# An early exponential for ScalarE's table, logits on two queues, halved matmuls in one half batch, and the last relus on VectorE, in a block-sorted attention with a top-1 expert layer

## The chip, the cores and the metric

The kernel runs on one core of one Trainium2 chip. The metric is the device time of one execution in microseconds (us). The kernel before took 153.61 us, the median of 3 runs (153.49 to 153.71). The profile shows one further execution, whose span from the first to the last instruction is 152.0 us.

## What is computed

The reference has two stages. The first is an attention in which the keys and values of each head are mixed over 8 blocks of 96 positions by a matrix P; P comes from five rounds of exponential, row normalisation and column normalisation of small logits (`sort_net`). The second sends each of the 3072 rows of the result to the one expert with the largest logit.

```python
B, H, S, D = 4, 8, 768, 64          # batch, heads, positions, head size
P = sort_net                        # (4, 8, 8, 8)
for _ in range(5):
    P = np.exp(P - np.max(P, axis=-1, keepdims=True))
    P = P / (np.sum(P, axis=-1, keepdims=True) + 1e-09)
    P = P / (np.sum(P, axis=-2, keepdims=True) + 1e-09)
k_sorted = einsum('bhij,bhjcd->bhicd', P, k_blocks)      # the same for v
attn = softmax(q_block @ k_sorted_block.T / sqrt(D))
x = (attn @ v_sorted_block)         # to (3072, 512)
logits = x @ w_gate                 # 8 experts
for e in range(8):                  # rows whose largest logit is e
    h = np.maximum(x[rows] @ w1[e], 0)                   # 512 -> 1024
    out[rows] = gate[rows] * (h @ w2[e])                 # 1024 -> 512
```

## The kernel before

The kernel does not write its instructions in a fixed order. It describes them as tasks, each with an assumed cost, the engines that could do it, its predecessors and a priority. A small planner inside the program places the tasks when the program is built: it assigns each to an engine and a time, tries 1500 random changes of the priorities from a fixed seed, keeps the changes that do not make the planned end later, and then emits the instructions in the order that it found. The program that reaches the chip is static. A changed cost or a changed choice of engine therefore changes the input of this search, and with it perhaps the order of every engine's instructions.

The planner guesses one expert for each batch ahead of time (a "vote" of summed values times the gate weights), so that this expert's weights can be loaded early; a branch after the last instruction repairs rows that went elsewhere, if there are any.

Where the plan leaves TensorE idle in the first 32 us, it puts in matmuls on a tile of zeros, whose results nobody reads:

```python
    def fill(self, t):
        at = self.free.get("pe", self.begin)
        while t.start < self.until and t.start - at > 0.5:
            n = self.grain if at < self.warm else 512
            free = [i for i in range(8) if self.bank[i] is not None and self.bank[i] <= at - 0.3]
            if not free:
                break
            t.spares.append((free[-1], n))
            ...
    # when the task is emitted
    for i, n in t.spares:
        nc.tensor.matmul(out=psum[:, i, :n], lhsT=idle[:, :128], rhs=idle[:, :n], start=True, stop=True)
```

The planner also counts TensorE's instructions, a matmul and its weight load as two, because it expects them to be fetched in blocks of 256 (`BLOCK_AT, BLOCK = 191, 256`), and it avoids runs of short instructions that would outpace the fetch.

The sort logits are loaded twice, into two groups of 32 partitions, both times from the sync queue; the gate weights come on ScalarE's queue. The five rounds then alternate between ScalarE (exponential) and VectorE (sum, reciprocal, product, once by rows and once by columns):

```python
    def load_sn(e, g):
        nc.sync.dma_start(out=sn[g * BH:(g + 1) * BH], in_=sort_net.rearrange("b h i j -> (b h) i j"))

    sn_at = [add(f"load sn{g}", {"sp": 0.4}, lambda e, g=g: load_sn(e, g), prio=-999, lands=0) for g in range(G)]
    wg_at = add("load wg", {"act": 1.75}, lambda e: nc.scalar.dma_start(
        out=wg32, in_=moe_w_gate.rearrange("(c p) e -> p c e", p=P)), prio=-998, lands=0)
    ...
    mk_idle = add("idle", {"dve": 0.27}, lambda e: nc.vector.memset(idle, 0.0), prio=-995)
    ...
    last = sn_at[0]
    for it in range(5):
        last = add(f"exp {it}", {"act": 0.26}, lambda e: nc.scalar.activation(sn, sn, ACT.Exp), [last, *sn_at], prio=-990)
        ...
        norm(sn, sn, it, "r")
        norm(sn.transpose([0, 2, 1]), sn.transpose([0, 2, 1]) if it < 4 else None, it, "c")
```

The end of the rounds (`sng`) gives the small matrices `pv0` and `pk0` with which TensorE sorts the values (16 groups of 32 matmuls in all, `v{b}.{g}`) and the keys (`k{b}.{g}`) of a batch. For the first batch the values are first rewritten in another order ("relay") by ScalarE, GpSimd or VectorE. The scores of a batch (`s`) need all of its query and key evictions, the products with the values (`a`) also those of the values.

```python
    t = add(f"k{b}.{g}", {"pe": 0.465}, run_k, [k_at[b][g], pk_at[b, 0], pk_at[b, 1], pads["ksT", i2], *scores_of.get(b - 2, [])], at,
            opens=kb, mode="col", n=16)
    ...
    ts = add(f"s{b}.{i}", {"pe": 0.178}, run_s, [*q_ev, *k_ev, ex_user[xi], pads["ex", xi]], ...)
    te = add(f"exp{b}.{i}", {"act": 0.82}, ...)
    ...
    later["vote pick0"].behind = later["k0.0"]      # the first batch's vote stands behind its first key sort
```

The expert layer of a half batch (384 rows) is 8 groups of 4 matmuls with 384 columns, each followed by a relu on ScalarE or VectorE, and then 3 tiles of 8 matmuls with 512 columns, each weighed by ScalarE or VectorE and stored. The first half of the first batch is cut into parts of 192 rows, and the very last tile of all into two halves of 256 columns.

```python
    def mm_outputs(ps, w2t, hT, s, lo, hi, d0=0, d1=MD):
        for fc in range(lo, hi):
            nc.tensor.matmul(out=ps, lhsT=hT[:, fc, s * P:(s + 1) * P], rhs=w2t[:, fc, d0:d1],
                             start=(fc == 0), stop=(fc == FC - 1))

    def relu(e, dst, src):
        if e == "act":
            nc.scalar.activation(dst, src, ACT.Relu)
        else:
            nc.vector.tensor_scalar_max(dst, src, 0.0)
    ...
    relus[r].append(add(f"relu{b}.{half}.{fc}.{r}", {"act": 0.5, "dve": 0.56}, ...))
```

Of the kernel before, what the change touches and what calls it, by code (L numbers as in the profile page):

```python
# [9 lines left out]
F32 = mybir.dt.float32  # L10
# [5 lines left out]
ACT = mybir.ActivationFunctionType  # L16
# [22 lines left out]
class Plan:  # L39
# [7 lines left out]


    FETCH = (3.9, 6.0)
    RING = 8  # L50
    BLOCK_AT, BLOCK, PACE, WAIT = 191, 256, 12.5, 300

# [12 lines left out]
    def add(self, name, cost, run, after=(), prio=0, opens=None, closes=None, lands=None,  # L65
            mode="full", n=0):
        t = Task(name, cost, run, after, prio, opens, closes, lands, mode, n)
        self.tasks.append(t)
        return t
# [43 lines left out]
    def fill(self, t):  # L113

        at = self.free.get("pe", self.begin)
        while t.start < self.until and t.start - at > 0.5:
            n = self.grain if at < self.warm else 512
            free = [i for i in range(8) if self.bank[i] is not None and self.bank[i] <= at - 0.3]
            if not free:
                break  # L120
            t.spares.append((free[-1], n))
            at += n * (0.00085 if at < self.warm else 0.00042)
            self.bank[free[-1]] = at - 0.3
# [191 lines left out]
def kernel(  # L315
# [11 lines left out]
    nc = tc.nc  # L327
    B, H, S, D = q.shape
    NB = sort_net.shape[-1]
    BLK = S // NB  # L330
    BH = B * H
    N, MD = out.shape
    E = moe_w_gate.shape[-1]
    F = moe_w1.shape[-1]
    P = 128
    DC = MD // P
    FC = F // P
# [9 lines left out]
    SUB = NH // P  # L347
# [9 lines left out]
    def bank(banks):  # L357
        return psum[:, banks.at, :]
# [5 lines left out]
    add = plan.add  # L364

    def sb(shape, dt, name):
        return consts.tile(shape, dt, name=name)
# [17 lines left out]
    w2s = [sb([P, FC, MD], BF16, f"w2_{i}") for i in range(2)]  # L385
    hTs = [sb([P, FC, NH], BF16, f"hT{i}") for i in range(3)]
    outs = sb([P, 4, MD], F32, "o")
    idle = sb([P, 512], BF16, "idle")

    G = 2  # L390
    sn = sb([G * BH, NB, NB], F32, "sn")
# [4 lines left out]
    wg = sb([P, DC, E], BF16, "wg")  # L396
# [37 lines left out]
    q_at, k_at, v_at, w1_at, w2_at = {}, {}, {}, {}, {}  # L434
# [30 lines left out]
    PIECES = 4  # L465
# [12 lines left out]


    def load_sn(e, g):  # L480
        nc.sync.dma_start(out=sn[g * BH:(g + 1) * BH], in_=sort_net.rearrange("b h i j -> (b h) i j"))

    plan.free["sp"], plan.free["act"] = 0.45, 0.9
    sn_at = [add(f"load sn{g}", {"sp": 0.4}, lambda e, g=g: load_sn(e, g), prio=-999, lands=0) for g in range(G)]
    wg_at = add("load wg", {"act": 1.75}, lambda e: nc.scalar.dma_start(
        out=wg32, in_=moe_w_gate.rearrange("(c p) e -> p c e", p=P)), prio=-998, lands=0)

    plan.free["pool"] = 1.4
# [4 lines left out]
    for t in FIRST_LOADS:  # L493
# [3 lines left out]
                  prio=FIRST + 4)  # L497
# [83 lines left out]
    ek1 = add("expand k", {"pool": 0.82}, lambda e: run_expand(expand_k, NB * CQ), [mk_ident], prio=FIRST + 10)  # L581
    ev1 = add("expand v", {"pool": 0.5}, lambda e: run_expand(expand_v, NB * 2), [mk_ident], prio=FIRST + 10)

    last = sn_at[0]
    for it in range(5):
        last = add(f"exp {it}", {"act": 0.26}, lambda e: nc.scalar.activation(sn, sn, ACT.Exp), [last, *sn_at], prio=-990)

# [408 lines left out]
            nc.tensor.matmul(out=ps, lhsT=w1t[:, dc, fc * P:(fc + 1) * P],  # L996
                             rhs=x[:, dc], start=(dc == 0), stop=(dc == DC - 1))

    def mm_outputs(ps, w2t, hT, s, lo, hi, d0=0, d1=MD):
        for fc in range(lo, hi):  # L1000
            nc.tensor.matmul(out=ps, lhsT=hT[:, fc, s * P:(s + 1) * P], rhs=w2t[:, fc, d0:d1],  # L1001
                             start=(fc == 0), stop=(fc == FC - 1))

    def relu(e, dst, src):
        if e == "act":
# [12 lines left out]


    TWICE = 20  # L1020
    FFN_BANKS, PARTS = None, 2

    def add_expert(b):
        A = SPAN * (b + 1)
        i2 = b % 2
        relu_of[b], outs_of[b] = [], []
        hs = []
        for half in range(2):
            hi = counts["hT"] % 3
            counts["hT"] += 1  # L1030
            hs.append(hi)
            parts = PARTS if b == half == 0 else 1
            n = NH // parts
            group = min(512 // n, 4)
            relus = [[] for _ in range(parts)]
            for r, fc in ((r, fc) for r in range(parts) for fc in range(0, FC, group)):
                pb = Banks(1, FFN_BANKS)
                lo = half * NH + r * n
                steps = NB // 2 // parts
                s0 = half * NB // 2 + r * steps  # L1040
                at = A + half * 50 + 25 * (r * FC + fc) / FC / parts

                def hidden(pb, n=n, group=group):
                    return bank(pb)[:, :group * n].rearrange("p (g n) -> p g n", g=group)

                def run_h(e, pb=pb, lo=lo, n=n, fc=fc, group=group, hidden=hidden):
                    for g in range(group):
                        mm_hidden(hidden(pb)[:, g], w1s[i2], columns(b, lo, n), fc + g)

                t = add(f"h{b}.{half}.{fc}.{r}", {"pe": group * (0.65 / parts + 0.015 * (parts > 1))}, run_h,  # L1050
                        [*w1_at[b][:2 if b == 0 and fc + group <= FC // 2 else PIECES], *turn_of[b][s0:s0 + steps], *(hT_user[hi] or [])],
                        at, opens=pb, n=group * DC)
                relus[r].append(add(f"relu{b}.{half}.{fc}.{r}", {"act": 0.5, "dve": 0.56},
                                 lambda e, fc=fc, hi=hi, pb=pb, r=r, n=n, group=group, hidden=hidden: relu(
                                     e, hTs[hi][:, fc:fc + group, r * n:(r + 1) * n], hidden(pb)),
                                 [t], at - 12, closes=pb))
            cut = len(relus[0]) // 2
            relu_of[b] += [t for got in relus for t in got]
            users = []
            for s in range(SUB):  # L1060
                t = half * SUB + s
                need = relus[s * P // n:((s + 1) * P - 1) // n + 1]
                oi = counts["o"] % 4
                counts["o"] += 1
                final = b == B - 1 and t == NTB - 1
                cuts = ((0, MD // 2, "act", "act"), (MD // 2, MD, "dve", "sp")) if final else ((0, MD, None, "sp"),)
                used = []
                for j, (lo, hi_, way, queue) in enumerate(cuts):
                    pb = Banks(1, FFN_BANKS)
                    us = 0.866 * (hi_ - lo) / MD  # L1070
                    t1 = add(f"o{b}.{half}.{s}a{j}", {"pe": us}, lambda e, s=s, hi=hi, pb=pb, lo=lo, hi_=hi_: mm_outputs(
                        bank(pb)[:, :hi_ - lo], w2s[i2], hTs[hi], s, 0, FC // 2, lo, hi_),
                        [*w2_at[b][:PIECES // 2], *[t for got in need for t in got[:cut]]], A + half * 50 + 25 + 25 * s / SUB, opens=pb, n=FC // 2)
                    t2 = add(f"o{b}.{half}.{s}b{j}", {"pe": us}, lambda e, s=s, hi=hi, pb=pb, lo=lo, hi_=hi_: mm_outputs(
                        bank(pb)[:, :hi_ - lo], w2s[i2], hTs[hi], s, FC // 2, FC, lo, hi_),
                        [t1, *w2_at[b][PIECES // 2:], *[t for got in need for t in got[cut:]]], A + half * 50 + 25 + 25 * s / SUB, n=FC // 2)
                    users.append(t2)
                    outs_of[b].append(t2)
                    cost = {e: c for e, c in evac(hi_ - lo, act=0.25 + (hi_ - lo) * 0.00086,
                                                  dve=0.2 + (hi_ - lo) * 0.00107).items() if way in (None, e)}  # L1080
                    tv = add(f"w{b}.{t}.{j}", cost, lambda e, lo=lo, hi_=hi_, oi=oi, t=t, pb=pb: weigh(
                        e, outs[:, oi, lo:hi_], bank(pb)[:, :hi_ - lo], gws[:, b, t:t + 1]),
                        [t2, route_at[b], *(out_user[oi] or [])], A + half * 50 + 25 * s / SUB, closes=pb)
                    dma = nc.scalar if queue == "act" else nc.sync
                    pieces = 2 if b * NTB + t < TWICE else 1

                    def run_st(e, lo=lo, hi_=hi_, oi=oi, t=t, dma=dma, pieces=pieces):
                        rows = P // pieces
                        for r in range(pieces):
                            dma.dma_start(out=out[out_rows(b, t), lo:hi_][r * rows:(r + 1) * rows],  # L1090
                                          in_=outs[r * rows:(r + 1) * rows, oi, lo:hi_])

                    used.append(add(f"st{b}.{t}.{j}", {queue: 0.36 * pieces}, run_st, [tv], A, lands=-(hi_ - lo) / MD / 4))
                out_user[oi] = used
            hT_user[hi] = users
# [50 lines left out]
        rest_i, bank(tot)[:, :1], -1.0, float(N), op0=ALU.mult, op1=ALU.add), [t2], 30, closes=tot)  # L1146


    spot = sb([1, 1], F32, "spot")
    for i in range(6):  # L1150
        add(f"spare dve{i}", {"dve": 0.5}, lambda e: [nc.vector.memset(spot, 0.0) for _ in range(8)],
            [route_at[B - 1]], SPAN * B + 55 + 5 * i)

    plan.search(rounds=1500, seed=7)
# [8 lines left out]
    with tc.If(rv > 0):  # L1163
        w1t, w2t, hT = w1s[0], w2s[0], hTs[0]
# [59 lines left out]
```

## Time and profile before

| Engine | busy, us | share of the span | instructions |
|---|---|---|---|
| TensorE matmuls | 140.8 | 93% | 2236 |
| TensorE weight loads | 96.7 | 64% | 2254 |
| VectorE | 88.0 | 58% | 270 |
| ScalarE | 99.7 | 66% | 160 |
| GpSimd | 67.2 | 44% | 127 |

In the profile PE is TensorE's matmuls, PEld its weight loads, DVE is VectorE, ACT ScalarE, POOL GpSimd and SP the sync engine; a letter q after a name is the engine's sequencer or queue. "L586" is line 586 of the kernel. A row of the timeline gives the start, the duration (of the whole merged row), the engine, the line, the operation, the tiles written and read, the number of instructions, and in square brackets how long the engine had been idle and what ended that wait. A row of the table by stretches gives the bounds and length of the stretch, the busy time and the instructions of the five engines, then the mean granted clock of TensorE as a share of the full one, the busy share of the DMA engines (its scale can pass 1), and GB/s.

Two things about the reading. The ends of matmuls are modelled, so a busy TensorE need not be a TensorE at its peak, and starts are the safer quantity. And a share of the whole span says little here, for the first 26 us and the remaining 126 us have different limits.

### The profile page before, as it was taken

To read this page: it belongs to the slowest core of one execution; us is meant where nothing else is said; L and a number is where in the kernel's file an instruction comes from. 1 tells how busy PE (TensorE), PEld (TensorE's weight loads), DVE (VectorE), ACT (ScalarE), POOL (GpSimd) and SP (SyncE) were. 2 spreads that over 40 slices of the span, in tenths; PEclk is the share of its full clock that TensorE was granted. 3 is DMA by queue.
4 is the path that set the end of the run, shared out by engine and by line. 5 is a ranking of instruction groups with operands and counts; after the bars stand their busy time and mean duration, and the time that the engine had idled before them with its cause. 6 is when DMAs were issued, how large, how long until landed. Compare 5 with 4: busy or idle time off the path is not lost. (4 is left out here: it accounts for less than half of the span.)

```text
span 152.0 us, 5435 instructions
## 1 busy us (share of the span) xinstructions
PE 140.8 (93%) x2236; PEld 96.7 (64%) x2254; DVE 88.0 (58%) x270; ACT 99.7 (66%) x160; POOL 67.2 (44%) x127
## 2 busy tenths in 40 slices
PE   6875998999999999999999999999999999999980
PEld 6653976995676567777557656967466566654550
DVE  1688848794674778768808657856053853552010
ACT  1838799863678979767488753868677465773440
POOL 6886099828892486992821990580000000000000
PEclk9999689999999999999999999999999999999999
DMA  2999079999999999999999999599953003331632
GB/s 25 184 214 201 14 95 164 205 220 206 217 239 236 249 213 240 233 228 223 213 208 246 257 206 229 103 162 196 195 121 71 4 0 73 69 73 69 137 134 80
DMA packets 15035, 24.52 MB, mean 161 GB/s; under 512 B 2080, under 2 KB 8224, under 8 KB 15008
## 3 DMA queue, kind: packets, MB, share of 16 engines
q0 software_dynamic: 10464, 17.83, 65.5%
q1 hardware_dynamic: 3872, 6.18, 14.9%
q8 instruction: 18, 0.29, 0.7%
q10 hardware_dynamic: 672, 0.15, 0.4%
q14 instruction: 9, 0.07, 0.1%
HBM read 35.68 MB, written 6.29 MB: 276 GB/s over the span
## 5 line engine op out<-in xcount | busy, mean ns | idle before, releaser
L996 PE MATMUL psum<-xT,w 128*128 128x384 bf16 (+1 forms) x288 | 48.4, 308 | 0.0
L1001 PE MATMUL psum<-w,hT 128*128 128x512 bf16 (+1 forms) x185 | 43.6, 370 | 1.2 <-issue 0.5
L1006 ACT ACTIVATE hT<-psum 128x384 bf16<-128x384 f32 x54 | 26.5, 491 | 12.9 <-PE psum L996 12.2
L996 PEld LDWEIGHTS <-w 128*128 128x128 bf16 x288 | 24.8, 97 | 12.1
L1001 PEld LDWEIGHTS <-hT 128*128 128x128 bf16 x200 | 18.2, 98 | 17.5
L1012 ACT ACTIVATE o<-psum,gws 128x512 f32<-128x512 f32 (+1 forms) x23 | 15.6, 678 | 20.4 <-PE psum L1001 18.4
L913 ACT ACTIVATE ex<-psum 128x768 bf16<-128x768 f32 x32 | 24.4, 810 | 0.8 <-PE psum L904 0.5
L931 DVE TENSOR_TENSOR xo<-psum,rec 96x512 bf16<-96x512 f32 x32 | 22.0, 686 | 1.1
L476 POOL DMA_DIRECT2D w<-in_moe_w_dram x16 | 11.7, 741 | 8.3 <-DVE xo L931 3.7
L425 ACT CAST vs<-psum 128x1024 bf16<-128x1024 f32 x12 | 12.2, 1019 | 2.9 <-PE psum L871 2.6
L930 DVE RECIPROCAL rec<-psum 96x8 f32<-96x8 f32 x32 | 6.4, 200 | 12.6 <-PE psum L920 12.3
L920 PEld LDWEIGHTS <-ex 128*128 128x128 bf16 x256 | 10.8, 97 | 3.3 <-ACT ex L913 0.6
L920 PE MATMUL psum<-vs,ex 128*128 128x65 bf16 x256 | 12.5, 193 | 0.4 <-ACT ex L913 0.2
L471 POOL DMA_DIRECT2D w<-in_moe_w_dram x16 | 9.5, 599 | 7.4 <-issue 4.8
L759 POOL TENSOR_TENSOR v_tmp<-vr 128x384 bf16<-128x384 bf16 x12 | 11.1, 959 | 1.4 <-DVE vr L737 1.4
L427 DVE COPY xT<-psum 128x384 bf16<-128x384 bf16 x22 | 7.8, 353 | 6.3 <-PE psum L939 5.7
L871 PE MATMUL psum<-pv,vr 128*64 128x64 bf16 x512 | 11.2, 203 | 0.0
L871 PEld LDWEIGHTS <-vr 128*64 128x64 bf16 x512 | 10.1, 118 | 1.5 <-issue 1.3
L427 DVE CAST ksT<-psum 128x1024 bf16<-128x1024 f32 (+1 forms) x7 | 8.0, 1146 | 4.7 <-PE psum L837 2.8
L939 PE MATMUL psum<-ident,xo 96*128 96x96 bf16 x128 | 10.6, 206 | 0.0
L939 PEld LDWEIGHTS <-xo 96*128 96x128 bf16 x128 | 8.1, 97 | 3.5
L129 PE MATMUL psum<-idle 128*128 128x80 bf16 (+1 forms) x76 | 8.5, 291 | 1.9 <-DVE idle L504 1.4
(110 smaller groups left out, 168.3 us busy)
## 6 DMA issues: line engine op xcount, KB each, us to landing
w<-in_moe_w_dram POOLq DMA_DIRECT2D x32, 256.0 KB, 9.0
out_dram<-o SPq DMA_DIRECT2D x41, 128.0 KB, 4.0
q_in<-in_q_dram POOLq DMA_DIRECT2D x4, 768.0 KB, 13.2
v_in<-in_v_dram POOLq DMA_DIRECT2D x4, 768.0 KB, 11.1
k_in<-in_k_dram POOLq DMA_DIRECT2D x3, 768.0 KB, 17.3
k_in<-in_k_dram POOLq DMA_DIRECT2D x3, 256.0 KB, 11.3
out_dram<-o SPq DMA_DIRECT2D x3, 256.0 KB, 2.6
out_dram<-o ACTq DMA_DIRECT2D x1, 128.0 KB, 3.4
```

The costliest lines, as they stand in the source:

```text
L425: nc.scalar.copy(dst, src)
L427: engines[e].tensor_copy(dst, src)
L476: nc.gpsimd.dma_start(out=w2s[i][:, at], in_=w2_r[bass.ds(ev, 1), :, at].rearrange("e p c d -> p (e c) d"))
L871: nc.tensor.matmul(out=t[f * HP:(f + 1) * HP, u, :], lhsT=vr[i2][:, d // 2, :, d % 2], rhs=pv[b][:, f * H:(f + 1) * H, :].rearrange("p h i ...
L913: te = add(f"exp{b}.{i}", {"act": 0.82}, lambda e, ex=ex, sbk=sbk: nc.scalar.activation(ex[:, :H * BLK].rearrange("p (t c) -> p t c", t=2) ...
L920: nc.tensor.matmul(out=av[:, h // 4, h % 4, :], lhsT=ex[:, h * BLK:h * BLK + P], rhs=vs[i2][:, h * NB + i, :D + 1], start=(h % 4 == 0), st ...
L931: nc.vector.tensor_mul(xo, av[:, :, :, :D], rec.to_broadcast([BLK, 2, 4, D]))
L939: nc.tensor.transpose(out=tp[:, dc, :], in_=xf[:, dc * P:(dc + 1) * P], identity=ident[:BLK, :BLK])
L996: nc.tensor.matmul(out=ps, lhsT=w1t[:, dc, fc * P:(fc + 1) * P], rhs=x[:, dc], start=(dc == 0), stop=(dc == DC - 1))
L1001: nc.tensor.matmul(out=ps, lhsT=hT[:, fc, s * P:(s + 1) * P], rhs=w2t[:, fc, d0:d1], start=(fc == 0), stop=(fc == FC - 1))
L1006: nc.scalar.activation(dst, src, ACT.Relu)
L1012: nc.scalar.activation(dst, src, ACT.Copy, scale=gw)
```

## The change

It has five parts.

1. A one-element exponential, which needs only the zeroed tile, is put ahead of the five rounds, so that ScalarE loads its table for the exponential while the logits are still on their way.
2. The second copy of the logits is started from ScalarE's queue instead of the sync queue, and the gate weights move to the sync queue.
3. The planner fills gaps of TensorE from 0.35 us on, instead of 0.5 us.
4. In the second half of the third batch (`SHORT = (2, 1)`), each matmul of 512 columns of the second expert product becomes two of 256.
5. The relus of the last batch may only go to VectorE. (The small tile `spot`, which fillers of VectorE at the end wrote, now belongs to part 1; those fillers write into the zero tile.)

```diff
+    GAP = 0.35
...
-        while t.start < self.until and t.start - at > 0.5:
+        while t.start < self.until and t.start - at > self.GAP:
...
-        nc.sync.dma_start(out=sn[g * BH:(g + 1) * BH], in_=sort_net.rearrange("b h i j -> (b h) i j"))
+        (nc.scalar if g else nc.sync).dma_start(out=sn[g * BH:(g + 1) * BH], in_=sort_net.rearrange("b h i j -> (b h) i j"))
...
-    sn_at = [add(f"load sn{g}", {"sp": 0.4}, lambda e, g=g: load_sn(e, g), prio=-999, lands=0) for g in range(G)]
-    wg_at = add("load wg", {"act": 1.75}, lambda e: nc.scalar.dma_start(
+    sn_at = [add(f"load sn{g}", {"act" if g else "sp": 0.4}, lambda e, g=g: load_sn(e, g), prio=-999, lands=0) for g in range(G)]
+    wg_at = add("load wg", {"sp": 0.4}, lambda e: nc.sync.dma_start(
...
-    last = sn_at[0]
+    spot = sb([1, 1], F32, "spot")
+    last = add("exp table", {"act": 1.5}, lambda e: nc.scalar.activation(spot, idle[:1, :1], ACT.Exp), [mk_idle], prio=-997)
...
-    def mm_outputs(ps, w2t, hT, s, lo, hi, d0=0, d1=MD):
+    def mm_outputs(ps, w2t, hT, s, lo, hi, d0=0, d1=MD, pieces=1):
+        n = (d1 - d0) // pieces
         for fc in range(lo, hi):
-            nc.tensor.matmul(out=ps, lhsT=hT[:, fc, s * P:(s + 1) * P], rhs=w2t[:, fc, d0:d1],
-                             start=(fc == 0), stop=(fc == FC - 1))
+            for i in range(pieces):
+                nc.tensor.matmul(out=ps[:, i * n:(i + 1) * n], lhsT=hT[:, fc, s * P:(s + 1) * P],
+                                 rhs=w2t[:, fc, d0 + i * n:d0 + (i + 1) * n],
+                                 start=(fc == i == 0), stop=(fc == FC - 1 and i == pieces - 1), skip_group_check=pieces > 1)
...
+    SHORT = (2, 1)
...
-                relus[r].append(add(f"relu{b}.{half}.{fc}.{r}", {"act": 0.5, "dve": 0.56},
+                relus[r].append(add(f"relu{b}.{half}.{fc}.{r}", {"dve": 0.56} if b == B - 1 else {"act": 0.5, "dve": 0.56},
...
+                short = 2 if b == SHORT[0] and half == SHORT[1] else 1
...                 # in t1 and t2: mm_outputs(..., short) and n=FC // 2 * short
...
-        add(f"spare dve{i}", {"dve": 0.5}, lambda e: [nc.vector.memset(spot, 0.0) for _ in range(8)],
+        add(f"spare dve{i}", {"dve": 0.5}, lambda e: [nc.vector.memset(idle[:1, :1], 0.0) for _ in range(8)],
```

More of the change, by code (lines that the diff above doesn't have):

```diff
@@ L1071, in add_expert @@
                     t1 = add(f"o{b}.{half}.{s}a{j}", {"pe": us}, lambda e, s=s, hi=hi, pb=pb, lo=lo, hi_=hi_: mm_outputs(
-                        bank(pb)[:, :hi_ - lo], w2s[i2], hTs[hi], s, 0, FC // 2, lo, hi_),
-                        [*w2_at[b][:PIECES // 2], *[t for got in need for t in got[:cut]]], A + half * 50 + 25 + 25 * s / SUB, opens=pb, n=FC // 2)
+                        bank(pb)[:, :hi_ - lo], w2s[i2], hTs[hi], s, 0, FC // 2, lo, hi_, short),
+                        [*w2_at[b][:PIECES // 2], *[t for got in need for t in got[:cut]]], A + half * 50 + 25 + 25 * s / SUB, opens=pb, n=FC // 2 * short)
                     t2 = add(f"o{b}.{half}.{s}b{j}", {"pe": us}, lambda e, s=s, hi=hi, pb=pb, lo=lo, hi_=hi_: mm_outputs(
-                        bank(pb)[:, :hi_ - lo], w2s[i2], hTs[hi], s, FC // 2, FC, lo, hi_),
-                        [t1, *w2_at[b][PIECES // 2:], *[t for got in need for t in got[cut:]]], A + half * 50 + 25 + 25 * s / SUB, n=FC // 2)
+                        bank(pb)[:, :hi_ - lo], w2s[i2], hTs[hi], s, FC // 2, FC, lo, hi_, short),
+                        [t1, *w2_at[b][PIECES // 2:], *[t for got in need for t in got[cut:]]], A + half * 50 + 25 + 25 * s / SUB, n=FC // 2 * short)
                     users.append(t2)
@@ L1146 @@
         rest_i, bank(tot)[:, :1], -1.0, float(N), op0=ALU.mult, op1=ALU.add), [t2], 30, closes=tot)
-    spot = sb([1, 1], F32, "spot")
     for i in range(6):
-        add(f"spare dve{i}", {"dve": 0.5}, lambda e: [nc.vector.memset(spot, 0.0) for _ in range(8)],
+        add(f"spare dve{i}", {"dve": 0.5}, lambda e: [nc.vector.memset(idle[:1, :1], 0.0) for _ in range(8)],
             [route_at[B - 1]], SPAN * B + 55 + 5 * i)
```

## The prediction, made before the changed kernel ran

> **What bounds the kernel now.** I read the table by stretches first, cut where the work changes, because the shares of the page mix a start that waits with a long stretch that does not.
>
> ```profile
> 6.10:16.40 10.30, 7.44 (x148) 5.00 (x150) 8.78 (x37) 6.54 (x13) 6.92 (x23) 1.00 1.01 187
> 16.40:19.80 3.40, 3.23 (x95) 3.27 (x96) 1.90 (x6) 2.40 (x3) 1.13 (x2) 0.50 0.02 5
> 19.80:26.10 6.30, 5.33 (x141) 4.07 (x139) 4.67 (x9) 6.17 (x9) 6.17 (x11) 1.00 1.01 140
> 26.10:147.70 121.60, 120.45 (x1801) 80.11 (x1814) 70.33 (x211) 81.83 (x134) 48.32 (x80) 1.00 0.84 170
> 147.70:152.00 4.30, 0.01 (x1) 0.00 (x0) 0.48 (x1) 0.00 (x0) 0.00 (x0) 1.00 0.35 118
> ```
>
> From 26.1 us, where the first expert matmul starts, to 147.7 TensorE is busy 120.45 of 121.60 us, and a few tenths of the rest are records that the trace lacks. Nothing else comes near: ScalarE has 81.83, VectorE 70.33. After that stand 4.30 us of last eviction and store. So the time is: when TensorE gets enough work to stay full, plus the work that is then left, plus a tail of 4.3 us. The change acts on the first term. In the start TensorE is busy for 7.44 of 10.30 us, dummies included; then come 3.40 us at half the clock (the column 0.50).
>
> What delays the start is seen in the timeline of the first 21 us and the waits before its rows:
>
> ```profile
> 1.00 0.86 SPq L481 DMA_DIRECT2D sn<-in_sort_net_dram  x2
> ...
> 3.31 1.28 ACT L586 ACT_TABLE_LOAD   x1 [3.31 <-DMA sn<-in_sort_net_dram]
> ...
> 4.60 0.26 ACT L586 ACTIVATE sn<-sn 64x64 f32<-64x64 f32 x1
> ...
> 12.23 0.76 PE L748 MATMUL psum<-vmask,v_in 128*128 128x8 bf16 x24
> ...
> 13.92 0.45 DVE L604 TENSOR_TENSOR sng<-sn,red 32x32 bf16<-32x32 f32 x2
> ...
> 14.43 0.24 PE L691 MATMUL psum<-sng,ev_first 64*128 64x8 bf16 x4 [1.44 <-DVE sng L604]
> ...
> 15.62 0.49 PEld L837 LDWEIGHTS <-k_in 128*64 128x64 bf16 x16
> ...
> 19.11 0.95 PE L837 MATMUL psum<-pk,k_in 128*64 128x128 bf16 x16
> ```
>
> The table load stands between the logits' landing (3.31) and the first exponential (4.60): 1.28 us on a serial chain. The chain ends with `sng` at 13.92 + 0.45 = 14.37, 9.77 us after its first exponential. TensorE waits 1.44 us for it and then does the value and key sorts at once. The third key sort stands at 19.11, the first scores at 21.01, the first expert matmul at 26.16.
>
> **What the Trainium skill says.** "ScalarE: Activation LUTs", section "What ACT_TABLE_LOAD costs", gives about 1283 ns for a load, and a drain of about 1380 ns more. This trace agrees on the first (1.28 us) and shows no drain: the exponential starts 0.01 us after the load. The exponential of the change needs the same set, so the load is moved, not added. "DMA: Bandwidth & Descriptors", section "Issuing engines are not separate DMA queues", says that starting transfers from several engines saves only the time of issuing them. Here that is half of 0.86 us. "TensorE: Matmul & The Clock Gate", section "What's actually happening", has a clock that is halved after a poorly used window of about 3.4 us. The trace fits: the clock falls at 16.37 us for 3.41 us, and in the 3.41 us before it the table by stretches has TensorE busy for only 1.97; the window before that, with 3.13, was followed by the full clock. "Runtime: NRT & Kernel Launch", section "Instruction fetch mechanics", has instructions fetched in blocks of 256. The page agrees in size: 18 packets on the instruction queue are 0.29 MB, so 16 KB each.
>
> **Part 1 and 2, the table and the queues.** The zero tile is ready at 1.12 + 0.27 = 1.39. ScalarE issues its copy of the logits from 1.00 to about 1.45, then loads the table until 1.45 + 1.28 = 2.73, and the tiny exponential may take 0.2 (the one of 64 elements takes 0.26): free at about 2.95. The logits: one transfer lands 1.7 us after its issue, so both are there at about 2.75 instead of 1.46 + 1.75 = 3.2. The first exponential moves from 4.60 to about 3.0, **1.6 us earlier**. If the rounds keep their 9.77 us, `sng` is done at 12.8. Then 14.37 no longer bounds; two transfers do. The values land at 12.2 (matmul at 12.23, released by the DMA). The three key copies are issued from 3.47 to 5.63 and land 10.9 to 11.6 us after their issue, so at about 14.4, 15.5 and 16.5. The first key sort can move from 15.65 to some 14.4, the third from 19.11 to some 16.6.
>
> The vote stands behind the first key sort, so it gains about 1.2 us, and the first expert's weights with it (issued at 18.67, the first pieces landed 4.3 to 4.8 us later, so by 24.2; then by 23.0). They were not the last to come: the transposed rows were evicted at 25.16 + 0.48 = 25.64. Those follow the first scores, and these follow the third key sort and its eviction (0.59 to 0.69): 16.6 + 0.35 + 0.65 = 17.6 at the earliest. But ScalarE and VectorE also have the other evictions and the relays then. From 12.2 on I count for ScalarE two relays (1.7), two value and two key evictions (2.0 + 1.6), and for VectorE from 12.8 on the small products (0.8), the vote (0.6), one query (1.2), two key (1.9) and one or two value evictions (1.2 to 2.4): they are done at about 17.5 and 18.5 to 19.7. So I put the first scores at 18.5 to 19, **2 to 2.5 us** ahead of 21.01.
>
> **Part 3, the dummies.** With the wait of 1.44 us gone or filled, the window before 16.37 should be used well enough, and the half clock should vanish. At half clock 3.41 us lost at most 1.7 us of TensorE's work, but this is no second gain: it lies inside the interval just counted, where evictions and landings set the pace (ScalarE waited 1.0 us there for TensorE, VectorE 1.8). It is what lets the 2 to 2.5 be had. A dummy of 512 columns costs 0.22 us if it meets ready work.
>
> **Part 4, halved matmuls.** 3 tiles x 8 = 24 matmuls become 48. In the last stretch of the trace, starts of 512-column matmuls lie 216 ns apart and those of 256 columns 109.5, so a pair costs 219: 24 x 3 ns = **0.07 us lost**. What it buys is position: 48 instructions more (a weight load with each) move the later fetch boundaries. In the kernel before I find no stall at a boundary worth more than 0.1 us after 26 us, so I credit nothing.
>
> **Part 5, the last relus.** A relu of 384 columns takes 0.49 us on ScalarE and 0.55 on VectorE. 16 of them leave ScalarE, at most 7.9 us, and make 8.9 us on VectorE, which is nearly idle at the end (9.23 us of wait before its last instruction). TensorE waited for neither there. Each relu is 0.06 us later, hidden behind other matmuls: zero, and the tail of 4.3 us stays.
>
> **Sum.** The long stretch begins 2 to 2.5 us earlier, with about the same work left; minus 0.07; minus what the plan gives back, since its search starts from other numbers. In the long stretch the old plan lost hardly anything that is visible, so a new one is likelier a little worse: 0.2 us or so. I choose a gain of 2.0: 153.6 - 2.0 = **151.6 us**.
>
> **Rivals.** (a) *The landings take the place of the table.* Keys land at 16.5 whatever ScalarE does, so if the evictions cannot follow, only the vote's 1.2 us or less is left: 152.4. For it: ScalarE is busy 6.17 of 6.30 us from 19.8 to 26.1, and an eviction-bound start shifts only by what the evictions gain. Against: VectorE idled 1.8 us there for TensorE. (b) *All gains add up*, 1.6 of the chain and 1.7 of the clock: 150.3. Against: both lie in the same stretch and the key transfers limit it. (c) *The search ends worse*, or a fetch boundary falls among short matmuls: then the long stretch grows by 1 to 2 us and the time stays at 152.5 to 154. For it: every order may change. Against: whoever chose the odd half batch of part 4 probably had a reason of this kind. (d) *The half clock only moves* into another stretch: 3.41 us at half the clock where TensorE is full cost 1.7 us, leaving 153.3.
>
> **Range and chances.** Between (a) 152.4 and (b) 150.3 lies most of it, with (c) and (d) as the tail upward: 150.5 to 152.9. Over 2% faster means under 150.54, a gain of 3.1, which needs (b): 0.17. Slower by over 2% needs an unlucky plan without the gain: 0.02. The rest is 0.81.
>
> **What would show it.** Right, if the table load starts at about 1.5 and the first exponential of 64 elements at about 3.0; `sng` done near 12.8; no row of the clock at 0.50 after 10 us; first scores before 19.2 and first expert matmul near 24; busy TensorE from there within 0.5 us of 120.45, and 4.3 us after the last matmul. It is wrong if the first scores stay after 20 (a), if the stretch from the first expert matmul to the last matmul is over a microsecond longer than 121.6 (c), or if a half clock shows up later (d).

## The result, and the profile after

The changed kernel takes **152.93 us** (median of 4 runs, 152.92 to 153.31) against 153.56 us before (153.49 to 153.71): a ratio of 0.9963, with an interval of 0.9946 to 0.9981. It is faster by 0.6 us, or 0.4%. The prediction was 151.6, with 150.5 to 152.9 as its range: the gain was a third of what I expected, and the time fell just outside the range.

The page of the profile shows a span of 151.4 us in place of 152.0. Of the table by stretches of the changed kernel, the rows that answer to those shown before (bounds, length, then busy time and instructions of PE, PEld, DVE, ACT, POOL, then granted clock, DMA share and GB/s):

```profile
14.98:18.81 3.83, 3.42 (x157) 3.21 (x151) 3.43 (x8) 3.61 (x5) 0.79 (x2) 1.00 0.18 29
18.81:21.81 3.00, 2.23 (x56) 1.68 (x56) 1.99 (x4) 3.00 (x5) 2.88 (x5) 1.00 0.70 97
21.81:25.22 3.41, 3.41 (x51) 2.49 (x45) 1.90 (x4) 2.42 (x4) 3.09 (x6) 0.50 1.11 159
25.36:140.46 115.10, 115.10 (x1824) 80.81 (x1822) 75.73 (x216) 71.21 (x111) 48.67 (x81) 1.00 0.87 173
140.46:141.08 0.62, 0.00 (x0) 0.00 (x0) 0.62 (x3) 0.00 (x0) 0.00 (x0) 1.00 0.15 30
147.74:151.40 3.66, 0.00 (x1) 0.00 (x0) 0.00 (x0) 0.47 (x1) 0.00 (x0) 1.00 0.38 133
```

Three things are to be seen. In this execution the half clock has not gone: it moved from 16.4 to 21.81 us. There is a new hole in TensorE's work at 140.46. And the tail is 3.66 us instead of 4.30. On the first of them the four executions of the comparison already say something: the profiled one, with a mean granted clock of 0.989, took 152.93 us, and the other three, with 0.995, 1.0 and 1.0, took 152.92, 152.92 and 153.31. The half clock came in one of the four and cost it nothing that shows. The timeline of the start (start, duration, engine, line, operation):

```profile
1.45 1.28 ACT L587 ACT_TABLE_LOAD   x1 [1.45 <-PEq L1216]
...
2.92 0.26 ACT L589 ACTIVATE sn<-sn 64x64 f32<-64x64 f32 x1
...
11.25 0.81 POOL L580 COPY expand_k<-ident 32x768 bf16<-32x768 bf16 x1
11.33 0.81 DVE L596 TENSOR_TENSOR sn<-sn,red 64x64 f32<-64x64 f32 x1
...
12.46 0.85 POOL L740 COPY vr<-v_in 128x384 uint32<-128x384 uint32 x1
...
12.70 1.00 DVE L607 TENSOR_TENSOR sng<-sn,red 32x32 bf16<-32x32 f32 x2
...
18.02 2.92 POOL L472 DMA_DIRECT2D w<-in_moe_w_dram  x4 [4.26 <-DVE vs L428]
...
18.81 0.52 PE L907 MATMUL psum<-qT,ksT 64*128 64x96 bf16 x16 [0.41 <-DVE ksT L428]
...
25.36 0.82 PE L999 MATMUL psum<-xT,w 128*128 128x192 bf16 x8
```

The table load now runs beside the logits' copies, and the first exponential moved by 1.68 us, from 4.60 to 2.92. But `sng` ends at 13.70, only 0.67 us earlier; the first expert's weights are issued at 18.02 in place of 18.67; and the first expert matmul moved from 26.16 to 25.36. The end, in the timeline:

```profile
138.27 1.70 DVE L1159 MEMSET idle<- 1x1 bf16 x15
140.01 0.55 DVE L1014 TENSOR_SCALAR hT<-psum 128x384 bf16<-128x384 f32 x1
...
141.08 1.46 PE L999 MATMUL psum<-xT,w 128*128 128x384 bf16 x8 [0.62 <-DVE hT L1014]
```

Fifteen filler memsets stand ahead of a relu that only VectorE may do now, and TensorE waits for the bank that this relu frees. So the span adds up: the first expert matmul 0.80 us earlier; from it to the end of the last matmul (147.74) 122.38 us in place of 121.55, so 0.83 given back; the tail 0.64 shorter. That is a gain of 0.6.

### The profile page after: what moved, and what is told of

Same layout as the page of the kernel before. It is cut to its first block, busy times and chain, and to the rows that moved or that the text cites. A ratio compares the mean times of both kernels' runs of the same rounds, so it can differ in the third digit from the quotient of the medians.

```text
span 151.4 us, 5564 instructions
## 1 busy us (share of the span) xinstructions
PE 142.4 (94%) x2305; PEld 100.7 (67%) x2305; DVE 97.4 (64%) x288; ACT 91.8 (61%) x143; POOL 67.1 (44%) x127
## 4 chain that ended last, share of the span: by engine, by line
PE 87%; DMA 5%; ACT 2%; DVE 2%; issue 1%; DVEq 0%; POOLq 0%
PE psum L999 28%; PE psum L1006 28%; PE psum L874 6%; PE psum L923 5%; PE psum L907 5%; DMA q_in<-in_q_dram 5%; PE psum L942 4%; PE psum L840 4%; PE psum L817 4%; PE psum L966 2%; ACT ex L916 1%; PE psum L130 1%; ACT qT L426 1%; DVE sn L596 1%; DVE ksT L428 0%
## 5 line engine op out<-in xcount | busy, mean ns | idle before, releaser
L1006 PE MATMUL psum<-w,hT 128*128 128x512 bf16 (+1 forms) x248 | 45.7, 331 | 0.0
L1006 PEld LDWEIGHTS <-hT 128*128 128x128 bf16 x248 | 23.0, 98 | 14.7
L1018 ACT ACTIVATE o<-psum,gws 128x512 f32<-128x512 f32 (+1 forms) x21 | 14.2, 677 | 27.3 <-PE psum L1006 16.7
L1012 ACT ACTIVATE hT<-psum 128x384 bf16<-128x384 f32 x36 | 17.7, 492 | 9.7 <-PE psum L999 8.8
L1014 DVE TENSOR_SCALAR hT<-psum 128x384 bf16<-128x384 f32 x28 | 15.1, 554 | 6.9 <-PE psum L999 6.7
L923 PE MATMUL psum<-vs,ex 128*128 128x65 bf16 x256 | 13.0, 196 | 0.3 <-ACT ex L916 0.3
L942 PE MATMUL psum<-ident,xo 96*128 96x96 bf16 x128 | 11.2, 211 | 0.0
L130 PE MATMUL psum<-idle 128*128 128x80 bf16 (+1 forms) x82 | 9.5, 291 | 1.4 <-DVE idle L505 1.4
L874 PEld LDWEIGHTS <-vr 128*64 128x64 bf16 x512 | 9.3, 112 | 1.5 <-issue 1.0
L874 PE MATMUL psum<-pv,vr 128*64 128x64 bf16 x512 | 10.2, 197 | 0.0
```

The costliest lines, as they stand in the source:

```text
L874: nc.tensor.matmul(out=t[f * HP:(f + 1) * HP, u, :], lhsT=vr[i2][:, d // 2, :, d % 2], rhs=pv[b][:, f * H:(f + 1) * H, :].rearrange("p h i ...
L923: nc.tensor.matmul(out=av[:, h // 4, h % 4, :], lhsT=ex[:, h * BLK:h * BLK + P], rhs=vs[i2][:, h * NB + i, :D + 1], start=(h % 4 == 0), st ...
L942: nc.tensor.transpose(out=tp[:, dc, :], in_=xf[:, dc * P:(dc + 1) * P], identity=ident[:BLK, :BLK])
L1006: nc.tensor.matmul(out=ps[:, i * n:(i + 1) * n], lhsT=hT[:, fc, s * P:(s + 1) * P], rhs=w2t[:, fc, d0 + i * n:d0 + (i + 1) * n], start=(fc ...
L1018: nc.scalar.activation(dst, src, ACT.Copy, scale=gw)
```

## The experiments

In all of them the edit stands after the planner's search or leaves the input of the search as it was. It changes only what is emitted, or moves the few tasks that it names, so that the rest of the order is that of the kernel that it starts from. Each run has a label, which is given with it; runs that start with b edit the kernel before, those that start with a the changed kernel. The runs were timed on three chips, in three sessions: b_early, b_short, a_nospare and a_warm; then a_same, a_pool, a_noshort and a_best; then a_vote, b_vote and a_best2. Each ratio is against the kernel before in the same session, and leaves out executions over 1.5% above the fastest of their kernel (one of a_nospare, three of b_vote, four of the kernel before in the third session), which the medians and ranges include. The median of the kernel before was 153.93, 154.29 and 154.58 us in the three sessions, against 153.56 in the first comparison. Its executions with a lower mean clock took longer: in the first session 153.40 to 153.95 us at 0.993 or more, and 154.41 to 154.64 at 0.984 or less. So the size of a gain depends on the session: the whole change reads 0.6 us in the first comparison and 1.3 us in the second session. Differences between sessions are weak evidence here, and what the timelines show is the stronger.

**Parts 1 and 2 alone** (b_early). The small exponential ahead of the first round, and the three copies on the new queues, in the kernel before.

```diff
+    def early_exp(e, run=named["exp 0"].run):
+        nc.scalar.activation(early, idle[:1, :1], ACT.Exp)
+        run(e)
+    named["exp 0"].run = early_exp      # and: logits' second copy on ScalarE's queue, gate weights on sync
```

> The kernel before, in its own order, with parts 1 and 2 alone: the small exponential stands just ahead of the first of the five rounds, the second copy of the logits comes on ScalarE's queue, the gate weights on the sync queue. Theory (the table's 1.6 us reach the end only in part, because GpSimd's copies then meet VectorE's last products, and the half clock comes in some other window): first exponential of the rounds at about 2.9 us, products of sng done at 12.8 to 13.7, first expert matmul 0.7 to 1.2 us before 26.16, time 152.4 to 152.9. Rival (landings and the vote bound the start, the table is hidden): first expert matmul less than 0.3 us earlier, time 153.3 to 153.6. Second rival (everything passes on): 1.5 us or more, time 152.1 or less.

152.78 us (152.41 to 153.39), ratio 0.9934 (0.9905 to 0.9963). First exponential at 2.87, `sng` done at 13.51: its pair of products took 1.49 us. The first expert matmul came at 23.92, 2.2 us earlier, better than the theory had it. But at 27.3 TensorE then waited 0.94 us for the weights, a wait that the kernel before doesn't have, and the last eviction began 1.10 us earlier (146.71 for 147.81). The clock stayed full in the profile. So neither number alone tells the gain: the scores gave 2.2 us, the weights took half back. The theory was right on the sum and wrong on its cause; the first rival was right that the landing of the weights bounds the start, and wrong that nothing would be left.

**Part 4 alone** (b_short). The split matmuls in the kernel before. (The split as written holds for both halves of the third batch: the functions that emit the matmuls read `short` only after the loop over the halves has ended, and it is 2 then. The profile of the changed kernel has 112 matmuls of 256 columns, 16 of them the final tile's. So 48 became 96, not 24 became 48.)

```diff
-                             rhs=w2t[:, fc, d0:d1], start=(fc == 0), stop=(fc == FC - 1))
+                                 rhs=w2t[:, fc, d0 + i * n:d0 + (i + 1) * n], ...)   # two of 256 columns, third batch
```

> The kernel before, in its own order, with part 4 alone as the change really emits it: 48 matmuls of 512 columns become 96 of 256, in both halves of the third batch. Theory (the tail after the last matmul is 0.64 us shorter in the changed kernel because the last instruction fetch, which came at 147.95 us beside the final stores, moves away from the end): last fetch 4 to 9 us before the last matmul ends, tail about 3.7 us in place of 4.3, TensorE 0.14 us longer, time 153.0 to 153.2. Rival (the tail is shorter because the other half of the final tile comes last, on the other queue): tail 4.3, time 153.7.

153.5 us (152.36 to 154.62), ratio 0.9969 (0.9942 to 0.9997). From the start of the last eviction to the end it is 3.19 us, against 4.19 in the kernel before. That fits the fetch theory and not the rival, for the same half tile comes last in both. In this profile the half clock lay from 14.9 to 18.3, the weights were issued 1.1 us late, and the last eviction began 1.26 us later than before; so the size of the gain isn't settled by this run, but its place is.

**The changed kernel without the filler memsets** (a_nospare).

```diff
+    for i in range(6):
+        named[f"spare dve{i}"].run = lambda e: None
```

> The changed kernel, in its own order, without the 48 one-element memsets that fill VectorE near the end. Theory (15 of them, 1.7 us, stand ahead of a relu that now only VectorE may do, and TensorE waits 0.78 us for its bank): no wait of TensorE near 140 us, time 152.1 to 152.3. Rival (VectorE alone is too slow for the relus): a wait of 0.4 us or more stays, time 152.6 or more. Should the memsets serve the end of the program in some way, the tail after the last matmul grows beyond 3.7 us.

152.25 us (151.89 to 154.75), ratio 0.9902 (0.9869 to 0.9935). The changed kernel itself was not timed on that chip; a_warm, which was and keeps the memsets, took 152.84, 0.6 us more. TensorE's wait near 140 us is gone: 22 matmuls run in a row from 137.74, and the five relus of that time take 3.16 us on VectorE without holding anybody. So VectorE alone is fast enough for the last relus; the memsets ahead of them were the cost.

**The changed kernel with five more dummies** (a_warm).

```diff
+    warm({"s0.0": 2, "s0.2": 1, "a0.1": 1, "s0.4": 1})     # dummies of 512 columns ahead of these tasks
```

> The changed kernel, in its own order, with five more dummy matmuls of 512 columns where TensorE was idle between 18.4 and 21.8 us (two before the first scores, three before later scores and products). Theory (the half clock from 21.81 to 25.22 us costs 0.5 to 0.8 us of the start): no record of half clock in 20 to 30 us, first expert matmul at 24.6 to 24.9 in place of 25.36, time 152.1 to 152.5. Rival (evictions and exponentials bound that stretch, the clock is hidden): first expert matmul within 0.2 us of 25.36 or later, time 152.8 to 153.1.

152.84 us (152.73 to 153.37), ratio 0.9934 (0.9911 to 0.9956). The half clock is gone in all 10 executions (mean granted clock 0.997 or more), and the first expert matmul came at 24.45, 0.9 us earlier. Yet TensorE then waited 0.5 us for the weights, and the time is in the rival's range and 0.1 us from the 152.93 of the first comparison, which was another session. With the executions of that comparison, which took no longer at 0.989 than at 1.0, this tells against my theory: the half clock costs 0.9 us of the scores, but not of the time.

**The changed kernel once more** (a_same), for its spread.

> The changed kernel unchanged, for its spread. Theory (TensorE's half clock comes by a window whose position differs from one execution to the next): executions with a mean granted clock near 0.989 take 0.3 to 0.8 us longer than those at 0.995 or more; median 152.8 to 153.1. Rival (the half clock at 21.8 us belongs to this kernel's order): the granted clock is 0.989 in nearly all.

153.03 us (152.72 to 153.32), ratio 0.9916 (0.9884 to 0.9947). All six executions had a mean clock of 0.996 or more, where the first profile had 0.989 (3.41 us at half in a span of 151.4 make 0.989): the half clock at 21.8 us is not fixed to this order. In the kernel before on this chip all 27 were at 0.994 or less. In the timeline of this run, without the half clock:

```profile
18.10 2.91 POOL L472 DMA_DIRECT2D w<-in_moe_w_dram  x4 [4.25 <-DVE vs L428]
18.89 1.39 PE L907 MATMUL psum<-qT,ksT 64*128 64x96 bf16 x32 [0.41 <-DVE ksT L428]
...
24.11 0.96 PE L999 MATMUL psum<-xT,w 128*128 128x192 bf16 x8
...
27.87 0.67 PE L999 MATMUL psum<-xT,w 128*128 128x192 bf16 x6 [1.18 <-DMA w<-in_moe_w_dram]
```

The first expert matmul stands at 24.11, where the prediction had put it. Then 1.18 us go to the weights. The span is 151.4 us, the same as with the half clock and no such wait: two delays side by side, and the longer one counts.

**GpSimd's copies out of the way** (a_pool).

```diff
+    named["expand k"].run = named["expand v"].run = lambda e: None
+    named["rev"].run = late       # rev, then both copies of expand, at some 26 us
```

> The changed kernel, in its own order, with GpSimd's two copies of expand (1.3 us, at 11.25 to 12.5 us) moved to some 26 us, after the issue of the first expert's weights; the work is the same. Theory (GpSimd's copies slow VectorE's two-input products: 0.81 us instead of 0.27, 1.00 instead of 0.45): the last full product of the rounds takes 0.27, the pair of sng 0.45 to 0.9 as it still meets the relay; sng done at 12.7 to 13.3 in place of 13.70, weights issued 0.4 to 0.9 us earlier, time 0.2 to 0.7 us below that of a_same. Rival (those products are long for another reason, such as the wait for ScalarE or a semaphore): they stay at 0.8 and 1.0, time that of a_same.

152.44 us (152.19 to 152.86), ratio 0.9882 (0.985 to 0.9914), 0.6 us below the changed kernel on the same chip. The timeline:

```profile
11.33 0.22 DVE L596 TENSOR_TENSOR sn<-sn,red 64x64 f32<-64x64 f32 x1
...
12.10 1.08 DVE L607 TENSOR_TENSOR sng<-sn,red 32x32 bf16<-32x32 f32 x2
12.25 0.85 POOL L740 COPY vr<-v_in 128x384 uint32<-128x384 uint32 x1 [0.96 <-DMA v_in<-in_v_dram]
```

The product that had taken 0.81 us beside the copy takes 0.22 without it; the pair of `sng`, which still meets the relay, takes 1.08. In the changed kernel the slow product ended at 12.14, 0.08 us after the copy did (11.25 + 0.81), and here the pair ends at 13.18, 0.08 us after the relay: in both cases the cost is about the rest of the copy. The Trainium skill, "SBUF — State Buffer", section "Who interferes with whom", says that a VectorE instruction with two SBUF inputs contends with a GpSimd instruction that reads SBUF, and that one with at most one SBUF input does not, outside the modes that use two ports. The traces agree: in the kernel before, the same copy of GpSimd (11.24 to 12.05) met a reduction of one input, which took its usual 0.26 us.

**The changed kernel without part 4** (a_noshort).

```diff
-                        bank(pb)[:, :hi_ - lo], w2s[i2], hTs[hi], s, 0, FC // 2, lo, hi_, short),
+                        bank(pb)[:, :hi_ - lo], w2s[i2], hTs[hi], s, 0, FC // 2, lo, hi_, 1),
```

> The changed kernel, in its own order, without part 4: the 96 matmuls of 256 columns are 48 of 512 again. Theory (part 4 moves the last instruction fetch away from the final stores): 96 instructions fewer bring that fetch to within 1 us of the last matmul's end, or past it; TensorE 0.14 us shorter, but the tail 4.2 to 4.4 us in place of 3.66; time 0.3 to 0.6 us above that of a_same. Rival (the tail is shorter because of which half of the final tile comes last): tail 3.7, time 0.14 us below.

153.39 us (152.94 to 154.84), ratio 0.9948 (0.9931 to 0.9965), 0.36 us above a_same. From the start of the last eviction to the end: 4.31 us, against 3.47 in a_same. The DMA views of the last 7 to 8 us show what lies there; first without part 4, then the changed kernel (queue, packets, MB, share; then the issues with their number, KB each and the median us to landing):

```profile
q8 instruction: 1, 0.02, 0.8%
out_dram<-o SPq DMA_DIRECT2D x2, 256.0 KB, 3.0
out_dram<-o SPq DMA_DIRECT2D x1, 128.0 KB, 3.5
out_dram<-o ACTq DMA_DIRECT2D x1, 128.0 KB, 2.8
```

```profile
q14 instruction: 1, 0.01, 0.3%
out_dram<-o SPq DMA_DIRECT2D x3, 256.0 KB, 2.1
out_dram<-o SPq DMA_DIRECT2D x1, 128.0 KB, 1.7
out_dram<-o ACTq DMA_DIRECT2D x1, 128.0 KB, 2.1
```

With one packet of q8 among them the last stores need 2.8 to 3.5 us to land, without it 1.7 to 2.1. I take q8 for TensorE's instruction queue: at 256 instructions each, as in the prediction, its 18 packets are 4608 instructions, and the profile of the changed kernel has 4610 of TensorE. (q14, the other instruction queue, has a packet there with and without part 4.) The same holds in all 13 profiles: in the four with the q8 packet among the last stores (the kernel before, b_early, b_vote and this one) they land in 2.7 to 3.6 us, in the nine without it in 1.7 to 2.4. With b_short this settles part 4: its 96 instructions move the last fetch from beside the final stores to 7 or 8 us before the last matmul ends (to 139.47 in the changed kernel). By the profiles that is worth 0.8 us, less an estimated 0.14 for the extra starts (48 at 3 ns). The medians show 0.36; the profiled execution took 153.74 us, 0.35 above its median, and the executions lie up to 1.9 us apart. How one fetch of 16 KB holds up these stores was not tried.

**Three repairs together** (a_best): no memsets, five dummies, the copies of expand moved.

> The changed kernel, in its own order, without the memsets of VectorE, with five more dummy matmuls between 18.4 and 21.8 us, and with the two copies of expand moved to some 26 us. Theory (the three losses are separate: 0.78 us at the end, up to 0.8 at the half clock, 0.5 by GpSimd's copies; the landing of the first expert's weights then bounds the first expert matmuls, and they come earlier with the vote): first expert matmul at 23.4 to 24.2, a wait for the weights of up to 0.7, time 151.0 to 151.7, that is 0.985 to 0.989 of the kernel before on a quiet chip. Rival (the weights' landing takes back what the copies give): 151.9 to 152.1.

151.58 us (151.31 to 152.38), ratio 0.9824 (0.9788 to 0.9859): 1.45 us below the changed kernel on the same chip. Weights issued at 17.54, a wait for them of 0.35 us, the first expert matmul at 24.08.

**The vote ahead**, in the changed kernel (a_vote) and in the kernel before (b_vote). Two tasks move; everything else keeps its order.

```diff
+    move("vote pick0", "v0.1")       # ahead of the first value and key sorts
+    move("vote read0", "q ev0.2")    # ahead of the third query eviction
```

> The changed kernel in its own order but for two tasks: the vote's last matmul stands ahead of the first value and key sorts, and VectorE reads it ahead of the third query eviction. The work is the same. Theory (the start of the changed kernel is bound by the landing of the first expert's weights, which follow the vote; this takes back what the earlier scores gave): weights issued at 16.9 to 17.2 us in place of 18.1, TensorE's wait for them at 27 us falls from 1.2 to 0.3 us or less, time 0.6 to 1.0 us below that of a_same (153.03), so 152.0 to 152.4. Rival (the exponentials and evictions bound it; the wait for weights only takes the place of another): time within 0.3 of a_same.

152.06 us (151.41 to 153.14), ratio 0.9862 (0.981 to 0.9913), 1.0 us under a_same, which ran in another session, or 0.8 by the two ratios. Its timeline:

```profile
24.15 0.82 PE L999 MATMUL psum<-xT,w 128*128 128x192 bf16 x8
...
26.84 0.67 PE L999 MATMUL psum<-xT,w 128*128 128x192 bf16 x6 [0.25 <-DMA w<-in_moe_w_dram]
```

The first expert matmul has not moved (24.11 in a_same), and the wait fell from 1.18 to 0.25. The two executions with a mean clock of 0.989 took 152.56 and 153.14, the four at full clock 151.41 to 152.18. That fits a half clock that costs time once the weights no longer hide it, though two executions are few.

> The kernel before in its own order with the same two tasks moved. There TensorE never waited for the weights in its profile. Theory (in the kernel before the late scores and the weights end together, the scores a little later, so that earlier weights alone give little): weights issued about 1 us earlier, first expert matmul within 0.5 us of 26.16, time within 0.4 us of the kernel before on the same chip. Rival (the vote alone bounded the start of both kernels): 0.7 us or more faster.

154.05 us (153.12 to 156.9), ratio 0.9975 (0.9946 to 1.0004); the weights issued at 17.55 instead of 18.67, the first expert matmul at 26.19, no wait for weights. So in the kernel before the same edit gives 0.4 us or nothing: there the scores were late too.

**Everything** (a_best2), and the relay of GpSimd held back until `sng` is done.

```diff
+    def relay_late(e, run=named["relay0.8"].run):
+        nc.gpsimd.tensor_copy(gate, sng[:1, 0, :2])     # waits for sng
+        run(e)
```

> The kernel a_best with the vote ahead as in a_vote, and with GpSimd's relay held back until the pair of sng is done, by a copy of two elements that reads sng. Theory: without a copy of GpSimd beside them, the pair of sng takes 0.45 us in place of 1.02 and ends at 12.5; weights issued at 15.7 to 16.2, no wait of TensorE for them, first expert matmul at 23.3 to 23.9, time 150.8 to 151.4. Rival (landing of the keys and the evictions bound it now): sng at 12.5, but first scores and time as in a_best (151.58), less 0.3 at most.

151.24 us (150.94 to 151.61), ratio 0.9804 (0.9763 to 0.9844). The pair of `sng` takes 0.47 us (12.22 to 12.69), and TensorE doesn't wait for weights. But the first scores stand at 18.68 and the first expert matmul at 24.19: the rival had that right. The third key sort at 17.06 waits 0.17 us for its keys, so the keys' landing, and with it the evictions, probably set the start now; no run tried that. The time is in the theory's range, 0.34 us under a_best of the session before. This is the fastest of all kernels here.

## Why the prediction was wrong

**The table and the queues** were right: load at 1.45 (about 1.5), first exponential at 2.92 (about 3.0), no added load.

**"If the rounds keep their 9.77 us"** failed: they took 10.78. Moved forward, the last products fell beside GpSimd's copies of expand and the relay, which stood at 11.24 and 12.46 in the timeline of the kernel before, too. `sng` came at 13.70, not 12.8. With these copies out of the way (a_best2) the rounds take 9.81 us again (2.88 to 12.69).

**"They were not the last to come"** is the step that cost most. I compared the landing of the first weights (4.3 to 4.8 us after issue) with the transposed rows, and stopped there. The third group of the expert's first matmuls needs all four pieces, the last of them from its third matmul on. In the kernel before (the issues from 20 us on with their time to landing, then the group):

```profile
L471 POOL DMA_DIRECT2D w<-in_moe_w_dram x2: 733/737/741, 20.1 to 20.9; - x2
DMA to landing us min/median/max: 7.4/7.4/7.5
...
28.27 0.83 PE L996 MATMUL psum<-xT,w 128*128 128x192 bf16 x8
```

The last piece was issued at 20.9 and landed at 28.3, just when that group began: weights and scores were even there, with no wait to be seen. In a_same the last piece came at 20.3 + 7.5 = 27.8; the group's first two matmuls ran at 26.35, and the other six stood at 27.87. So the change moved the scores by 2.2 us (18.81, inside the "18.5 to 19" of the prediction) and the weights by 0.65. The vote's gain of "about 1.2 us" was 0.65 because the late `sng` delayed the first key sort as well (14.97, not 14.4). So the start gained about what the weights gained, 0.65 to 0.8 us, with the half clock or without: rival (a) in its mechanism, though it named the keys' landing and not the weights'. The vote ahead shows it from both sides: weights 1.1 us earlier moved that group by 1.0 us in the changed kernel (27.87 to 26.84) and not at all in the kernel before (28.27 to 28.30).

**"The half clock should vanish"** failed in the profiled execution and held in the other three of the comparison, by their mean clock, and in all six of a_same. Where it failed, rival (d) came true, but not its 1.7 us, since the weights hid it. In the 3.41 us before the clock fell, TensorE was busy 2.23 us; in the kernel before 1.97. It stayed full after a window with 2.27 there and one with 2.44 here. Parts 1 and 2 alone, without part 3, had a mean clock of 0.994 or more in all 7 executions, so the earlier sort seems to do most of what I gave to the dummies. Part 3 alone was not tried.

**"Zero" for part 5** failed: 0.62 us of wait, or 0.78 counted from the start of one matmul to the start of the next (0.947 in place of 0.163 us). My argument rested on VectorE's idle time and not on what stands in its order. The memsets had been harmless while ScalarE did the relus. It is rival (c) in a small form: the stretch from the first expert matmul to the last grew by 0.83 us.

**"I credit nothing" for part 4** failed, and so did "the tail of 4.3 us stays": the tail is 0.6 us shorter, and 0.8 to 1.0 by the two runs that change part 4 alone. My argument was on stalls of TensorE at a fetch, and not on what the last fetch lies beside. My 0.07 of cost becomes 0.14 by the same estimate, since twice as many matmuls are split.

In one sum: 2.0 predicted, less 1.2 for weights that I had not followed to the last piece, less 0.8 for the stretch with the memsets, plus 0.6 for the tail, gives 0.6. The last two nearly cancel, which is luck: I had both at about zero. What the new order as such is worth, and part 5 in the old order, was not tried.

## What to carry to other kernels

When a chain gets shorter, list every other input of the stage that it feeds, each to its last piece: the gain ends at the second latest. Something that stood harmlessly beside an old place, a copy on the other engine, filler in an in-order queue, can lie on the path in the new one, and it can be read from the old timeline. To learn what a part is worth in a kernel whose order comes from a search, fix the order and change only what is emitted.

## What the runs showed that I had not expected

A product of VectorE with two inputs took 0.81 us beside a copy of GpSimd and 0.22 without it. TensorE's clock was halved for 3.41 us after a stretch of 3.41 us in which it had been busy for 2.23 us, and whether and where that happens differs from one execution to the next: six executions of the changed kernel on one chip had no such stretch by their mean clock, and of two programs that are the same up to the third batch's expert, one had it from 16.4 us and the other from 14.9. And where one instruction fetch lay beside the last stores, they landed in 2.7 to 3.6 us instead of 1.7 to 2.4.
